# Gate and value products of eight of twelve row blocks in seven-product form, in an attention and SwiGLU kernel on one core

## The chip, the core and the metric

The kernel runs on one core of a Trainium2 chip. Its engines work side by side and wait for each other by semaphores: TensorE (PE; its weight loads are PEld) multiplies matrices into PSUM banks, ScalarE (ACT) and VectorE (DVE) move and combine what lies in PSUM and SBUF, GpSimd (POOL) here computes on tiles in SBUF alone and issues some DMA, SyncE (SP) issues the other DMA. The "granted clock" is the share of TensorE's full speed that the profile records as granted to it. The metric is the device time of one execution in microseconds, median of several.

## The reference

Linear attention (8 batches, 8 heads, 576 tokens, head size 64) gives x, and a SwiGLU block is applied to it:

```python
q_s = softmax(q, axis=-1);  k_s = softmax(k, axis=2)          # shapes 8, 8, 576, 64
kv  = einsum('bhsd,bhse->bhde', k_s, v)
x   = einsum('bhsd,bhde->bhse', q_s, kv)  -> (4608 tokens, 512)
g   = x @ w_gate                                              # 512 x 1536
out = (g * sigmoid(g) * (x @ w_val)) @ w_out                  # 1536 x 512, fp32
```

## The kernel before

The 1536 hidden features are 12 row blocks of 128; 512 tokens are one chunk. For each row block a unit makes gate and value by eight 512-column matmuls, Silu on ACT, and the product on DVE:

```python
def m_unit(c0, n, m):
    ...
    for w, nm in ((wg, "g_ps"), (wv, "u_ps")):
        ps = [f_tile(nm) for _ in parts]
        for kk in range(KT):                                  # KT = 4
            for p_, (c, w_) in zip(ps, parts):
                nc.tensor.matmul(out=p_[:, 0:w_], lhsT=w[:, kk, ms], rhs=xt[:, kk, c:c + w_], ...)
    ...
        nc.scalar.activation(out=sg[:, 0:w_], in_=g_ps[:, 0:w_], func=AF.Silu)
        nc.vector.tensor_mul(hr[:, m, r:r + w_], sg[:, 0:w_], u_ps[:, 0:w_])
```

The output product already has seven-product form (Strassen's scheme in Winograd's variant): `o_quad` needs seven block products instead of eight, four sums of the weights (`w_sums`, once, on POOL) and four sums of h in each chunk:

```python
def h_sum(Q, i, ...):          # a[t][c]: token half t, feature half c of h
    if i == 0:   eng.tensor_add(s[0], a[1][0], a[1][1])
    elif i == 1: eng.tensor_sub(s[1], s[0], a[0][0])
    elif i == 2: eng.tensor_sub(s[2], a[0][0], a[1][0])
    else:        eng.tensor_sub(s[3], a[0][1], s[1])
```

In the kernel before, the four h sums stand on DVE behind the units 0 to 3, one each, and the chunk's attention work stands between other units. The kernel's PSUM pool has eight buffers, called banks in what follows, and every PSUM tile takes one. Names in the traces below: `qs` is the softmax of q, `kv` the product of keys and values, `kn` the same, normalised, `xa` and `xz` the banks in which x arises, `xt` x in SBUF, `vb` the 16-bit copy of v.

The softmax here doesn't subtract the row's maximum and nothing guards it: scores larger than these inputs give would overflow.

## Time and profile before

| | before |
|---|---|
| median of 3 runs | 310.19 us (309.98 to 310.38) |
| span of the profiled run | 308.0 us |
| PE / DVE / ACT / POOL busy | 98 / 66 / 47 / 18 % |
| one 512-token chunk with attention | 31.9 us |

From the page of the kernel before, the table of busy time (us, share of the span, instructions) and the chain of waits (share of the span of each engine on the chain that ended last):

```profile
PE 302.4 (98%) x2200; PEld 183.1 (59%) x2200; DVE 204.1 (66%) x395; ACT 144.1 (47%) x232; POOL 55.7 (18%) x42
...
PE 93%; DVE 4%; DMA 1%; ACT 0%; issue 0%
```

TensorE bounds it, nearly without a gap. The timeline of the kernel before, PE alone, gives the price of a matmul (columns: start, duration, engine, line, operation, output and inputs, shapes, count; us):

```profile
120.82 1.47 PE L383 MATMUL ox<-wt,hr 128*128 128x256 f16 x12
122.13 1.03 PE L304 MATMUL g_ps<-xt,wg 128*128 128x512 bf16 x4
122.99 1.03 PE L304 MATMUL u_ps<-xt,wv 128*128 128x512 bf16 x4
```

Read starts, not durations, since the ends are modelled and overlap. Twelve matmuls of 256 columns take 122.13 - 120.82 = 1.31 us, 109 ns each; four of 512 take 0.865 us, 216 ns each. Per column they cost the same, so fewer columns is less time.

Timeline of the kernel before, DVE and POOL only, where h sums on DVE met POOL; the last line is an h sum that met nothing:

```profile
74.22 3.09 POOL L351 TENSOR_TENSOR wt<-wo,wt 128x1536 f16<-128x1536 f16 x1
...
76.78 1.34 DVE L361 TENSOR_TENSOR hs<-hr 128x1536 bf16<-128x1536 bf16 x1
...
77.26 1.87 POOL L112 CAST vb<-v 128x1152 bf16<-128x1152 f32 x1
...
78.65 1.29 DVE L363 TENSOR_TENSOR hs<-hs,hr 128x1536 bf16<-128x1536 bf16 x1
...
79.72 1.23 POOL L112 CAST vb<-v 128x1152 bf16<-128x1152 f32 x1 [0.59 <-DMA v<-in_v_dram]
...
80.46 1.29 DVE L365 TENSOR_TENSOR hs<-hr 128x1536 bf16<-128x1536 bf16 x1
...
108.66 0.95 DVE L361 TENSOR_TENSOR hs<-hr 128x1536 bf16<-128x1536 bf16 x1
```

Add start and duration. POOL ends at 77.31, the sum at 78.12; POOL at 79.13, the sum at 79.94; POOL at 80.95, the sum at 81.75. Each time DVE ends 0.80 to 0.81 us after POOL, whenever it began. Two engines that shared a rate would not give a constant; one that waits for the other's end does. The four later h sums of this profile that met POOL (from 112.11, 143.98, 175.85 and 207.72 us) also ended 0.81 us after it. In the other direction, the cast at 77.26 ends 1.01 us after the DVE sum at 78.12.

### The profile page before, as it was taken

Reading aid. Unit: us, or ns where it says so; the run is one execution under the profiler, and the core shown is the slowest. Engines: PE = TensorE matmul, PEld = TensorE weight load, DVE = VectorE, ACT = ScalarE, POOL = GpSimd, SP = SyncE. Lnnn points to the kernel's source line nnn. Section 1 sums busy time; section 2 is a strip of 40 time slices with the busy share of each in tenths; the row PEclk is TensorE's granted clock in tenths of the full one; section 3 lists DMA queues with packets and bytes.
Section 4 is the critical chain, followed back from the end, with each engine's and each line's share of the span. In section 5 each row is a group of like instructions: output and inputs, shape, how many; then the busy total and the mean of one; then the engine's idle time right before and its main releaser. Section 6 shows DMA issues by size and latency. Waiting matters only on the chain.

```text
span 308.0 us, 5679 instructions
## 1 busy us (share of the span) xinstructions
PE 302.4 (98%) x2200; PEld 183.1 (59%) x2200; DVE 204.1 (66%) x395; ACT 144.1 (47%) x232; POOL 55.7 (18%) x42
## 2 busy tenths in 40 slices
PE   8999999999999999999999999999999999999994
PEld 6777855454675458455844485448544764485443
DVE  3944459967867886788687768776877653664422
ACT  4753387824493439333944385347634213322300
POOL 1840014189420121102020302020200000000000
PEclk9999999999999999999999999999999999999999
DMA  7999999749019910894089506960540050006014
GB/s 262 263 185 207 250 393 391 221 89 393 24 31 203 385 59 0 177 321 180 0 165 294 217 2 144 285 247 2 119 97 0 0 121 19 0 2 136 3 34 103
DMA packets 39180, 46.39 MB, mean 151 GB/s; under 512 B 16368, under 2 KB 22384, under 8 KB 39152
## 3 DMA queue, kind: packets, MB, share of 16 engines
q1 hardware_dynamic: 33104, 41.17, 45.6%
q0 software_dynamic: 5808, 4.72, 9.8%
q8 instruction: 17, 0.28, 0.4%
q10 hardware_dynamic: 240, 0.13, 0.2%
q14 instruction: 11, 0.09, 0.1%
HBM read 37.75 MB, written 9.44 MB: 153 GB/s over the span
## 4 chain that ended last, share of the span: by engine, by line
PE 93%; DVE 4%; DMA 1%; ACT 0%; issue 0%
PE g_ps L304 31%; PE u_ps L304 30%; PE ox L383 12%; PE ow L383 6%; PE o_ps L331 5%; PE oy L383 3%; PE kv L190 3%; DMA q<-in_q_dram 1%; DVE rs L137 1%; PE o_ps L445 1%; PE xa L272 1%; DVE qs L146 1%; DVE xt L232 0%; DVE qt L112 0%; PE xz L272 0%; ACT eq L121 0%
## 5 line engine op out<-in xcount | busy, mean ns | idle before, releaser
L312 ACT ACTIVATE sg<-g_ps 128x512 f32<-128x512 f32 (+2 forms) x120 | 65.1, 554 | 124.3 <-PE g_ps L304 116.9
L313 DVE TENSOR_TENSOR hr<-sg,u_ps 128x512 bf16<-128x512 f32 (+2 forms) x120 | 74.2, 631 | 60.9 <-PE u_ps L304 60.4
L304 PE MATMUL g_ps<-xt,wg 128*128 128x512 bf16 (+2 forms) x480 | 111.6, 358 | 0.2
L304 PE MATMUL u_ps<-xt,wv 128*128 128x512 bf16 (+2 forms) x480 | 111.0, 358 | 0.0
L304 PEld LDWEIGHTS <-wv 128*128 128x128 f16 x480 | 46.9, 98 | 46.9 <-issue 0.3
L304 PEld LDWEIGHTS <-wg 128*128 128x128 f16 x480 | 45.9, 98 | 44.8 <-issue 2.2
L112 POOL CAST vb<-v 128x1152 bf16<-128x1152 f32 x14 | 19.6, 1398 | 103.5 <-DMA v<-in_v_dram 42.2
L383 PEld LDWEIGHTS <-hs 128*128 128x128 bf16 x336 | 32.9, 98 | 3.8
L383 PEld LDWEIGHTS <-hr 128*128 128x128 bf16 x252 | 24.7, 98 | 4.3
L137 DVE TENSOR_REDUCE rs<-eq 128x18 f32<-128x1152 bf16 x16 | 21.5, 1346 | 6.3 <-ACT eq L121 6.3
L146 POOL TENSOR_TENSOR qs<-eq,rr 128x1152 bf16<-128x1152 bf16 x7 | 14.8, 2121 | 58.2 <-DVE rr L141 49.1
L383 PE MATMUL ox<-wt,hs 128*128 128x256 f16 x168 | 20.6, 273 | 0.0
L121 ACT ACTIVATE eq<-q 128x1152 bf16<-128x1152 f32 x16 | 18.0, 1158 | 2.7 <-DMA q<-in_q_dram 2.6
L121 ACT ACTIVATE ek<-k 128x1152 bf16<-128x1152 f32 x16 | 18.0, 1152 | 2.0 <-DMA k<-in_k_dram 2.0
L331 PE MATMUL o_ps<-wo,hr 128*128 128x512 f16 x84 | 18.8, 379 | 0.0
L214 DVE TENSOR_SCALAR kn<-kv,kvr 64x64 bf16<-64x64 f32 x56 | 15.9, 283 | 1.3
L417 DVE COPY s<-ox 128x256 f32<-128x256 f32 x14 | 5.9, 425 | 12.8 <-PE ox L383 12.8
L146 DVE TENSOR_TENSOR qs<-eq,rr 128x1152 bf16<-128x1152 bf16 x9 | 13.5, 1498 | 0.4 <-DVE rr L141 0.2
L331 PEld LDWEIGHTS <-hr 128*128 128x128 bf16 x84 | 8.1, 98 | 9.5 <-issue 0.2
L255 PE MATMUL warm_ps<-zero 128*128 128x256 bf16 x80 | 11.2, 307 | 1.1 <-DVE zero L464 1.1
L190 PEld LDWEIGHTS <-ek 64*128 64x128 bf16 x288 | 8.4, 94 | 3.6 <-issue 2.5
L255 PEld LDWEIGHTS <-zero 128*128 128x128 bf16 x80 | 8.6, 110 | 3.1 <-DVE zero L464 1.1
(61 smaller groups left out, 230.8 us busy)
## 6 DMA issues: line engine op xcount, KB each, us to landing
q<-in_q_dram SPq DMA_DIRECT2D x16, 576.0 KB, 7.1
k<-in_k_dram SPq DMA_DIRECT2D x16, 576.0 KB, 8.5
v<-in_v_dram SPq DMA_DIRECT2D x16, 576.0 KB, 9.5
out_dram<-o_sb SPq DMA_DIRECT2D x70, 128.0 KB, 2.4
wo<-in_moe_w_out_dram POOLq DMA_DIRECT2D x3, 512.0 KB, 18.0
wg<-in_moe_w_gate_dram POOLq DMA_DIRECT2D x2, 512.0 KB, 11.1
wv<-in_moe_w_val_dram POOLq DMA_DIRECT2D x2, 512.0 KB, 12.8
wg<-in_moe_w_gate_dram POOLq DMA_DIRECT2D x2, 256.0 KB, 5.3
```

Source lines behind the costliest of these rows:

```text
L112: eng.tensor_copy(out=out, in_=in_)
L121: nc.scalar.activation(out=s["e" + what], in_=raw[what, b, G].rearrange("p h (t d) -> p t h d", d=64), func=AF.Exp,)
L137: nc.vector.reduce_sum(out=rs, in_=s["eq"].rearrange("p t h d -> p (t h) d"), axis=mybir.AxisListType.X)
L146: eng.tensor_mul(s["qs"].rearrange("p t (h d) -> p (t h) d", d=64), s["eq"].rearrange("p t h d -> p (t h) d"), s["rr"].to_broadcast([128, ...
L190: nc.tensor.matmul(out=s["kv"][g][:, 0:129], lhsT=s["ek"][r, t, :, :].rearrange("p h d -> p (h d)"), rhs=s["vb"][r, t, 0:129], start=(t == 0),
L214: nc.vector.tensor_scalar_mul(out_, src, sc)
L255: nc.tensor.matmul(out=ps[:, 0:256], lhsT=zero[:, 0:128], rhs=zero, start=True, stop=True)
L304: nc.tensor.matmul(out=p_[:, 0:w_], lhsT=w[:, kk, ms], rhs=xt[:, kk, c:c + w_], start=(kk == 0), stop=(kk == KT - 1),)
L312: nc.scalar.activation(out=sg[:, 0:w_], in_=g_ps[:, 0:w_], func=AF.Silu)
L313: nc.vector.tensor_mul(hr[:, m, r:r + w_], sg[:, 0:w_], u_ps[:, 0:w_])
L331: nc.tensor.matmul(out=o_ps, lhsT=hr[:, m, r0:r0 + 128], rhs=wo[:, m, :], start=(m == 0), stop=(m == MT - 1),)
L383: nc.tensor.matmul(out=dst[p][:, 0:HN], lhsT=lhs(kk, p), rhs=rhs(kk), start=start and kk == 0, stop=kk == HM - 1, skip_group_check=True,)
```

## The change

The intent is to do to gate and value what `o_quad` does to the output: token halves (t = 0, 1) and halves of the 512 inputs make the left operand, halves of the inputs and gate | value the right one. Seven products of two row blocks cost 7 x 4 matmuls of 256 columns, where direct form costs 16 of 512, that is one eighth less. Four "cycles" a chunk each do two row blocks so, and weave one direct row block in, so that ACT and DVE have time to empty the banks. Cut to its core:

```diff
-    xt = const.tile([128, KT, n_tok], BF16, name="xt", tag="xt")
+    xt = const.tile([128, KT, XR], FP16, name="xt", tag="xt")          # XR = 1536, a ring
+    gt = const.tile([128, 4, 2, SD], FP16, name="gt", tag="gt")        # weight sums
+    xs = [const.tile([128, 2, 256], FP16, ...) for i in range(4)]      # x sums
...
+    def g_sums(eng):        # four differences of gate and value weights, 128x2048 each
+    def x_sum(c0, i, eng=nc.vector):   # four sums of x, 128x512 each
+    def cycle(c0, n, mid=None, slot=None, late=None):
+        prod(bx, wg[:, 0:2], xa(0, 0), True)
+        nc.scalar.copy(out=s1, in_=bx)
+        prod(by, wg[:, 2:4], xa(0, 1), True)
+        prod(bw, gt[:, 0], xs[0], True)
+        nc.scalar.copy(out=s5, in_=bw)
+        flush()                                  # last product of the cycle before
+        nc.vector.tensor_add(s1, by, s1)
+        nc.scalar.activation(out=sa, in_=s1, func=AF.Silu)
+        ... mid(), slot()
+        direct(wg, g_ps)
+        prod(bx, gt[:, 1], xs[1])
+        nc.scalar.copy(out=s2, in_=bx)
+        nc.scalar.activation(out=sd, in_=g_ps, func=AF.Silu)
+        prod(bw, wv[:, 2:4], xs[3])
+        nc.vector.tensor_add(s2, bw, s2)
+        nc.gpsimd.tensor_mul(h_out(0), halves(sa), halves(s2))
+        direct(wv, u_ps)
+        prod(bx, gt[:, 2], xs[2])
+        nc.vector.tensor_add(s5, bx, s5)
+        nc.vector.tensor_mul(hr[:, md, rh:rh + 512], sd, u_ps)
+        ... late()
+        def last():
+            prod(bx, gt[:, 3], xa(1, 1))
+            nc.scalar.activation(out=sb, in_=bx, func=AF.Silu)
+            nc.gpsimd.tensor_mul(h_out(1), halves(sb), halves(s5))
+        pend.append(last)
...
     def o_quad(Q, between):
         ... first output product
+        between(-1)                              # flush()
         ... second output product
...
+        w_adds = g_sums(nc.vector)               # in the 448-token chunk:
+            if 4 <= m < 8:
+                w_adds[m - 4]()
...
+            def sums_h():
+                for i, eng in enumerate((nc.vector, nc.vector, nc.gpsimd, nc.gpsimd)):
+                    h_sum(ci, i, eng=eng)
+            cycle(c0, 0, slot=sums_h)
+            o_quad(ci, between)
+            cycle(c0, 1, slot=norm_1 if att else None)
+            cycle(c0, 2, mid=(lambda: kv_pair(b)) if att else None)
+            cycle(c0, 3, late=sums_x if ci + 1 < n_ch else None)
```

Left out of the cut: `kn` is made by one instruction for a 128x128 block, one `qs` multiply a chunk goes from DVE to POOL, v is loaded into two buffers instead of three, and in the 448-token chunk the x products stand one row block earlier.

The bank `bx` collects four products in turn. The "flushed product" is the last of them. It may start only when DVE's `s5` add has read the bank.

More of the change, by code (lines that the diff above doesn't have):

```diff
@@ L49 @@
     HN = d_model // 2
+    XR = 1536
+    NS = 4
+    SD = 2 * NS * 128
     WARM = (64, 8, 8)
@@ L54 @@
     at = ctx.enter_context(tc.tile_pool(name="at", bufs=2))
-    ff = ctx.enter_context(tc.tile_pool(name="ff", bufs=3))
+    ff = ctx.enter_context(tc.tile_pool(name="ff", bufs=4))
     ob = ctx.enter_context(tc.tile_pool(name="ob", bufs=5))
-    sn = ctx.enter_context(tc.tile_pool(name="sn", bufs=1))
+    sn = ctx.enter_context(tc.tile_pool(name="sn", bufs=2))
     psp = ctx.enter_context(tc.tile_pool(name="psp", bufs=8, space=bass.MemoryType.PSUM))
@@ L67 @@
     hs = const.tile([128, 4, HM, 256], BF16, name="hs", tag="hs")
-    xt = const.tile([128, KT, n_tok], BF16, name="xt", tag="xt")
+    xt = const.tile([128, KT, XR], FP16, name="xt", tag="xt")
+    gt = const.tile([128, 4, 2, SD], FP16, name="gt", tag="gt")
+    xs = [const.tile([128, 2, 256], FP16, name=f"xs{i}", tag=f"xs{i}") for i in range(4)]
     hr = const.tile([128, MT, RING], BF16, name="hr", tag="hr")
@@ L76, in load @@
     def load(b, G, what, src, after=None):
-        raw[what, b, G] = ld.tile([128, 2, T * 64], FP32, tag=what, name=what)
+        raw[what, b, G] = ld.tile(
+            [128, 2, T * 64], FP32, tag=what, name=what, bufs=2 if what == "v" else 3
+        )
         ap = bass.AP(
@@ L206, in kn, with ring_parts, put_x @@
         if "kn" not in s:
-            s["kn"] = at.tile([128, 2, 64], BF16, tag="kn", name="kn")
-        for h in range(2):
-            r = slice(64 * h, 64 * h + 64)
-            out_, src, sc = s["kn"][r, g, :], s["kv"][g][r, r], s["kvr"][r, g:g + 1]
-            if eng is nc.scalar:
-                nc.scalar.mul(out_, src, sc)
-            else:
-                nc.vector.tensor_scalar_mul(out_, src, sc)
+            s["kn"] = at.tile([128, 2, 128], BF16, tag="kn", name="kn")
+        out_, src, sc = s["kn"][:, g, :], s["kv"][g][:, 0:128], s["kvr"][:, g:g + 1]
+        if eng is nc.scalar:
+            nc.scalar.mul(out_, src, sc)
+        else:
+            nc.vector.tensor_scalar_mul(out_, src, sc)
+    def ring_parts(c0, n, ring):
+        c1 = c0 + n
+        while c0 < c1:
+            w_ = min(c1, (c0 // ring + 1) * ring) - c0
+            yield c0 % ring, w_
+            c0 += w_
+    def put_x(eng, k0, c0, src):
+        o = 0
+        for r, w_ in ring_parts(c0, src.shape[-1], XR):
+            copy(eng, xt[:, k0, r:r + w_], src[:, o:o + w_])
+            o += w_
     def x(b, G, piece, eng=nc.scalar):
@@ L225, in x @@
                     out=xp[h][64 * g:64 * g + 64, 0:n].rearrange("p (t c) -> p t c", c=64),
-                    lhsT=s["kn"][r, g, :],
+                    lhsT=s["kn"][r, g, r],
                     rhs=s["qt"][g][r, t0:t1, :],
@@ L230, in x @@
         c0 = b * S + 64 * t0
-        copy(eng, xt[:, 2 * G, c0:c0 + n], xp[0][:, 0:n])
-        nc.vector.tensor_copy(out=xt[:, 2 * G + 1, c0:c0 + n], in_=xp[1][:, 0:n])
+        put_x(eng, 2 * G, c0, xp[0][:, 0:n])
+        put_x(nc.vector, 2 * G + 1, c0, xp[1][:, 0:n])
     def x_both(b, G, eng=nc.scalar):
@@ L273, in x_pair @@
                             out=o[64 * g:64 * g + 64, :].rearrange("p (t c) -> p t c", c=64),
-                            lhsT=s["kn"][r, g, :],
+                            lhsT=s["kn"][r, g, r],
                             rhs=s["qt"][g][r, t0:t1, :],
@@ L278, in x_pair @@
             for h, eng in ((0, nc.scalar), (1, nc.vector)):
-                copy(eng, xt[:, 2 * G + h, c0:c0 + n_a], ps[G][h][:, 0:n_a])
+                put_x(eng, 2 * G + h, c0, ps[G][h][:, 0:n_a])
         for h, eng in ((0, nc.scalar), (1, nc.vector)):
-            copy(
-                eng,
-                xt[:, h:h + 2 * NG - 1:2, c0 + n_a:c0 + S],
-                z[h].rearrange("p (g c) -> p g c", g=NG),
-            )
+            o = 0
+            for r, w_ in ring_parts(c0 + n_a, n_z, XR):
+                copy(
+                    eng,
+                    xt[:, h:h + 2 * NG - 1:2, r:r + w_],
+                    z[h].rearrange("p (g c) -> p g c", g=NG)[:, :, o:o + w_],
+                )
+                o += w_
     def kv_pair(b):
@@ L304, in m_unit @@
                     nc.tensor.matmul(
-                        out=p_[:, 0:w_], lhsT=w[:, kk, ms], rhs=xt[:, kk, c:c + w_],
+                        out=p_[:, 0:w_], lhsT=w[:, kk, ms], rhs=xt[:, kk, c % XR:c % XR + w_],
                         start=(kk == 0), stop=(kk == KT - 1),
@@ L313, in m_unit, with flush @@
             nc.vector.tensor_mul(hr[:, m, r:r + w_], sg[:, 0:w_], u_ps[:, 0:w_])
+    pend = []
+    def flush():
+        while pend:
+            pend.pop()()
+    def g_sums(eng):
+        b11, b12 = wg[:, 0:2, 0:SD], wv[:, 0:2, 0:SD]
+        b21, b22 = wg[:, 2:4, 0:SD], wv[:, 2:4, 0:SD]
+        return [
+            lambda: eng.tensor_sub(gt[:, 0], b12, b11),
+            lambda: eng.tensor_sub(gt[:, 1], b22, gt[:, 0]),
+            lambda: eng.tensor_sub(gt[:, 2], b22, b12),
+            lambda: eng.tensor_sub(gt[:, 3], b21, gt[:, 1]),
+        ]
@@ new lines, in x_sum, with halves, prod, direct @@
+    def x_sum(c0, i, eng=nc.vector):
+        r = c0 % XR
+        a11, a12 = xt[:, 0:2, r:r + 256], xt[:, 2:4, r:r + 256]
+        a21, a22 = xt[:, 0:2, r + 256:r + 512], xt[:, 2:4, r + 256:r + 512]
+        if i == 0:
+            eng.tensor_add(xs[0], a21, a22)
+        elif i == 1:
+            eng.tensor_sub(xs[1], xs[0], a11)
+        elif i == 2:
+            eng.tensor_sub(xs[2], a11, a21)
+        else:
+            eng.tensor_sub(xs[3], a12, xs[1])
+    def cycle(c0, n, mid=None, slot=None, late=None):
+        r, rh = c0 % XR, c0 % RING
+        m0, md = 2 * n, 2 * NS + n
+        def halves(t):
+            return t.rearrange("p (j c) -> p j c", j=2)
+        def prod(bank, wgt, rhs, first=False):
+            for j in range(2):
+                c = slice(128 * (m0 + j), 128 * (m0 + j) + 128)
+                for kk in range(2):
+                    nc.tensor.matmul(
+                        out=bank[:, 256 * j:256 * j + 256], lhsT=wgt[:, kk, c], rhs=rhs[:, kk, :],
+                        start=first and j == 0 and kk == 0, stop=kk == 1, skip_group_check=True,
+                    )
+        def direct(w, ps):
+            for kk in range(KT):
+                nc.tensor.matmul(
+                    out=ps, lhsT=w[:, kk, 128 * md:128 * md + 128], rhs=xt[:, kk, r:r + 512],
+                    start=(kk == 0), stop=(kk == KT - 1),
+                )
+        def xa(t, c):
+            return xt[:, 2 * c:2 * c + 2, r + 256 * t:r + 256 * t + 256]
+        def h_out(t):
+            return hr[:, m0:m0 + 2, rh + 256 * t:rh + 256 * t + 256]
+        def sg_tile():
+            return ff.tile([128, 512], FP32, tag="sg", name="sg")
+        bx, by, bw = [f_tile(n_) for n_ in ("sx", "sy", "sw")]
+        s1, s2, s5 = [sn.tile([128, 512], FP32, tag=n_, name=n_) for n_ in ("s1", "s2", "s5")]
+        prod(bx, wg[:, 0:2], xa(0, 0), True)
[5 more added lines that the diff above has]
+        nc.vector.tensor_add(s1, by, s1)
+        sa = sg_tile()
+        nc.scalar.activation(out=sa, in_=s1, func=AF.Silu)
+        if mid is not None:
+            mid()
+        if slot is not None:
+            slot()
+        g_ps, u_ps = f_tile("g_ps"), f_tile("u_ps")
+        direct(wg, g_ps)
+        prod(bx, gt[:, 1], xs[1])
+        nc.scalar.copy(out=s2, in_=bx)
+        sd = sg_tile()
+        nc.scalar.activation(out=sd, in_=g_ps, func=AF.Silu)
[6 more added lines that the diff above has]
+        nc.vector.tensor_mul(hr[:, md, rh:rh + 512], sd, u_ps)
+        if late is not None:
+            late()
+        def last():
+            prod(bx, gt[:, 3], xa(1, 1))
+            sb = sg_tile()
+            nc.scalar.activation(out=sb, in_=bx, func=AF.Silu)
+            nc.gpsimd.tensor_mul(h_out(1), halves(sb), halves(s5))
+        pend.append(last)
@@ L372, in o_quad @@
         s1, s2, s5 = [
-            [sn.tile([128, HN], FP32, tag=f"{n}{p}", name=n) for p in range(2)]
-            for n in ("s1", "s2", "s5")
+            [t[:, HN * p:HN * p + HN] for p in range(2)]
+            for t in [sn.tile([128, 512], FP32, tag=n, name=n) for n in ("s1", "s2", "s5")]
         ]
@@ L549 @@
         exp(2, 1, "k")
-        chunks = [(S, 448)] + [(c, 512) for c in range(1024, n_tok, 512)]
-        for ci, (c0, n) in enumerate(chunks):
-            b = ci + 2
-            steps = {}
-            if b < B:
-                steps = {8: lambda: kv_pair(b), 10: lambda: x_pair(b)}
+        w_adds = g_sums(nc.vector)
+        for m in range(MT):
+            if m == 4:
+                norm_sum(2, 1)
+                norm_mul(2, 1, nc.gpsimd)
+                tr_dma(2, 1)
+                load_group(3, 0)
+                load_group(3, 1)
+            m_unit(S, 1024 - S, m)
+            if m == 5:
+                w_sums(nc.gpsimd)
+            if m == 8:
+                kv_pair(2)
+            if m == 9:
+                x_pair(2)
+            if 4 <= m < 8:
+                w_adds[m - 4]()
+        for i in range(4):
+            x_sum(1024, i)
+        n_ch = n_tok // 512 - 1
+        for ci in range(1, n_ch):
+            b, c0 = ci + 2, 512 * (ci + 1)
+            att = b < B
             def between(i):
-                if b >= B:
-                    return
-                if i == 0:
+                if i < 0:
+                    flush()
+                elif att and i == 0:
                     for G in range(NG):
@@ L565, in between, with norm_1, sums_x @@
                         cast_v(b, G, nc.gpsimd)
-                else:
+                elif att:
                     norm_sum(b, 0)
                     norm_mul(b, 0, nc.gpsimd)
-            for m in range(MT):
-                if ci == 0 and m == 4:
-                    norm_sum(2, 1)
-                    norm_mul(2, 1, nc.gpsimd)
-                    tr_dma(2, 1)
-                    load_group(3, 0)
-                    load_group(3, 1)
-                if ci > 0 and m == 4:
-                    o_quad(ci, between)
-                    if b < B:
-                        tr_dma(b, 0)
-                if ci > 0 and m == 5 and b < B:
-                    norm(b, 1)
-                    tr_dma(b, 1)
-                    if b + 1 < B:
-                        load_group(b + 1, 0)
-                        load_group(b + 1, 1)
-                m_unit(c0, n, m)
-                if ci == 0 and m == 5:
-                    w_sums(nc.gpsimd)
-                if ci > 0 and m < 4:
-                    h_sum(ci, m)
-                if m in steps:
-                    steps[m]()
+            def sums_h():
+                for i, eng in enumerate((nc.vector, nc.vector, nc.gpsimd, nc.gpsimd)):
+                    h_sum(ci, i, eng=eng)
+            def norm_1():
+                norm_sum(b, 1)
+                norm_mul(b, 1, nc.gpsimd)
+                tr_dma(b, 1)
+                if b + 1 < B:
+                    load_group(b + 1, 0)
+                    load_group(b + 1, 1)
+            def sums_x():
+                for i in range(4):
+                    x_sum(c0 + 512, i)
+            cycle(c0, 0, slot=sums_h)
+            o_quad(ci, between)
+            if att:
+                tr_dma(b, 0)
+            cycle(c0, 1, slot=norm_1 if att else None)
+            cycle(c0, 2, mid=(lambda: kv_pair(b)) if att else None)
+            if att:
+                x_pair(b)
+            cycle(c0, 3, late=sums_x if ci + 1 < n_ch else None)
+        flush()
         last = n_tok // 128 - 4
```

## The prediction

> **What bounds the kernel now.** TensorE: the page gives PE 302.4 of 308.0 us (98%), the chain of waits is 93% PE, at full granted clock. Timeline: four 512-column matmuls take 0.865 us, twelve 256-column ones 1.31 us (109 ns each; the 98 ns weight loads hide). A 512-token chunk with attention takes 31.9 us: 24 x 0.865 gate/value, 9.17 output products, 1.8 attention.
>
> **What the change removes.** In each of seven 512-token chunks eight row blocks cost 4 x 28 x 0.109 = 12.2 us instead of 13.8: 11.3 us in all. Without stalls: 299 us.
>
> **What it adds.** ACT: PSUM copies (0.58 each). DVE: adds (0.69), four x sums a chunk (estimate 0.45 each), four weight sums (estimate 1.2 each, from 0.95 for 1536). POOL: multiplies (estimate 1.05, from 3.09 for 1536) and half of the h sums (3.09 each).
>
> **Why I expect a loss.** The Trainium skill, "SBUF — State Buffer", section "Who interferes with whom", says a DVE instruction with two SBUF inputs and a GpSimd instruction reading SBUF exclude each other for a whole instruction. It agrees here: four h sums on DVE that met a busy POOL ended 0.80 to 0.81 us after POOL's op (1.34, 1.29, 1.29, 1.04 us instead of 0.95), and POOL casts that met DVE ended 1.0 us after it (1.87 to 2.01 instead of 1.14). Multiplies with one PSUM input did not slow.
>
> 1. Remainder chunk (448 tokens): four weight sums on DVE stand between the multiplies of row blocks 4 to 7 while POOL runs its four 3.09 us output-weight sums. They alternate, each holding DVE up to 4 us. PSUM banks come free late, and the kn products behind them hold back the x products: about 13 us of TensorE stall, plus 2 to 3 us at a lower clock after a 7 us gap.
> 2. Later chunks, cycle 0: flushed product, ACT Silu (0.6), POOL multiply (1.05); then POOL takes its h sum (3.09) before DVE's first h sum, which waits for it; only after two h sums come DVE's adds s2 and s5. The product flushed inside the output products needs s5: 4.0 us late, six chunks.
> 3. The x sums stand behind cycle 3's last multiply: the next chunk's third product waits 1.3 us.
> 4. Cycle 1: two table loads (1.28) and four exps leave ACT late for the s2 copy: 0.8 us; elsewhere 0.4.
>
> All of it is critical: TensorE runs in order. A full chunk: 30.1 + 1.3 + 4.0 + 1.2 = 36.6 us, against 31.9. Total: 13 to 15 (1) + 0.6 (first seven-product chunk) + 4 x 4.8 + 2 x 3.8 + 2 (final flush, clock) = 43 to 45 us; I shade it to 40.
>
> **Predicted: 350 us, 80% range 328 to 366. Faster by over 2%: 0.07; within 2%: 0.05; slower by over 2%: 0.88.**
>
> **What would show it.** PE busy 86 to 90%. Step 1: DVE weight sums of 2 to 4 us, TensorE waits of several us at 68 to 85 us. Step 2: the first h sum on DVE about 3.9 us long, the flushed product waiting 4 us for s5. Step 3: 1.3 us waits for the first x sum. Chunks of 36 to 37 us. Matmuls unchanged.
>
> **What would make it wrong.** DVE getting the port before POOL's h sum: step 2 shrinks to about 1.3 us, the whole lands near 325. Both locks absent: about 308. Gaps lowering the clock everywhere: over 366.

## The result, and the profile after

| | before | after |
|---|---|---|
| median | 310.09 us (4 runs) | 357.35 us (4 runs, 356.54 to 359.54) |
| ratio | | 1.153 (95% interval 1.148 to 1.159): slower |
| PE / DVE / ACT / POOL busy | 98 / 66 / 47 / 18 % | 86 / 65 / 52 / 51 % |
| mean granted clock | 1.00 | 0.957 |
| one chunk with attention | 31.9 us | 38.0 us (37.97 to 39.14 in four chunks) |

Ratios here and below are the mean time of one kernel's fast runs over that of the other's fast runs of the same rounds, so not quite the ratio of the medians quoted.

Page of the changed kernel, the same two lines as before, and the granted clock in tenths over 40 slices between them:

```profile
PE 306.4 (86%) x2536; PEld 220.8 (62%) x2536; DVE 231.1 (65%) x411; ACT 185.5 (52%) x315; POOL 181.5 (51%) x117
...
PEclk9999999978999989998999879998999899989999
...
PE 62%; DVE 14%; issue 7%; ACT 5%; POOL 5%; DMA 4%; SPq 1%; DVEq 0%; POOLq 0%; ACTq 0%
```

TensorE is busy no less, though it has fewer columns to do, because part of its work now runs at a lower clock; and 48 us of the span it is idle. The view of waits of the changed kernel, PE alone, says for what (us in total, times, longest):

```profile
PE sx L376 <- DVE s L423: 24.3, 7, 3.9
PE xa L290 <- DVE kn L219: 7.1, 1, 7.1
PE sw L376 <- DVE xs L357: 5.8, 7, 0.9
PE sx L376 <- ACT s L415: 2.7, 5, 0.5
PE g_ps L325 <- DVE hr L334: 1.5, 1, 1.5
```

The first line is the flushed product waiting for s5, the second and fifth the 448-token chunk, the third the x sums, the fourth the s2 copy of cycle 1. How the first comes about, in the timeline of the changed kernel (PE, DVE, POOL) through cycle 0 of one chunk and the start of its output products; brackets give idle time before and what ended it:

```profile
119.52 1.27 POOL L432 TENSOR_TENSOR hr<-sg,s 128x512 bf16<-128x512 f32 x1 [2.63 <-ACT sg L431]
...
120.74 3.09 POOL L486 TENSOR_TENSOR hs<-hr 128x1536 bf16<-128x1536 bf16 x1
120.82 3.83 DVE L482 TENSOR_TENSOR hs<-hr 128x1536 bf16<-128x1536 bf16 x1 [1.49 <-POOL hr L432]
...
121.57 1.47 PE L504 MATMUL ox<-wo,hr 128*128 128x256 f16 x12
...
124.68 0.96 DVE L484 TENSOR_TENSOR hs<-hs,hr 128x1536 bf16<-128x1536 bf16 x1
125.56 0.68 DVE L419 TENSOR_TENSOR s<-sw,s 128x512 f32<-128x512 f32 x1
...
126.16 0.68 DVE L423 TENSOR_TENSOR s<-sx,s 128x512 f32<-128x512 f32 x1
...
126.89 1.01 PE L376 MATMUL sx<-xt,gt 128*128 128x256 f16 x4 [3.85 <-DVE s L423]
127.70 2.77 PE L504 MATMUL ow<-wt,hs 128*128 128x256 f16 x12
```

POOL's multiply ends at 120.79. Its next instruction, the third h sum, begins at once; DVE's first h sum, which waited for the same multiply, begins 0.08 us later and ends at 124.65, which is 0.82 us after POOL's end at 123.83. DVE's instructions start in the order of the program, so both adds stand behind it (125.56 and 126.16), and TensorE waits 3.85 us. DVE shows "busy" for those 3.83 us; nothing in the busy share tells that it is blocked. Last line: the next twelve matmuls need 2.56 us (to the following start at 130.26) instead of 1.31, so the wait also cost clock.

The 448-token chunk of the changed kernel, DVE and POOL, shows the same lock among the weight sums:

```profile
62.37 2.12 POOL L153 TENSOR_TENSOR qs<-eq,rr 128x1152 bf16<-128x1152 bf16 x1 [3.61 <-DVE rr L148]
...
62.61 2.96 DVE L346 TENSOR_TENSOR gt<-wv,wg 128x2048 f16<-128x2048 f16 x1
...
64.45 4.06 POOL L469 TENSOR_TENSOR wt<-wo 128x1536 f16<-128x1536 f16 x1
...
66.02 3.58 DVE L347 TENSOR_TENSOR gt<-wv,gt 128x2048 f16<-128x2048 f16 x1
...
68.59 3.95 POOL L470 TENSOR_TENSOR wt<-wo,wt 128x1536 f16<-128x1536 f16 x1
...
70.05 3.58 DVE L348 TENSOR_TENSOR gt<-wv 128x2048 f16<-128x2048 f16 x1
```

The ends alternate: POOL 64.49, DVE 65.57, POOL 68.51, DVE 69.60, POOL 72.54, DVE 73.63. Each instruction runs only when the other engine's is done. Behind these sums stand the multiplies that free PSUM banks and the kn products that x needs. The seven-product stage starts at 84.43 us, where the kernel before starts its first 512-token chunk at 74.18. Part of this is clock: after the wait of 7.1 us four matmuls of 448 columns took 1.46 us and the next four 1.15 us, by their starts, instead of 0.76.

### The profile page after: what moved, and what is told of

Same layout as the page of the kernel before. It is cut to its first block, busy times and chain, and to the rows that moved or that the text cites. A ratio compares the mean times of both kernels' runs of the same rounds, so it can differ in the third digit from the quotient of the medians.

```text
span 354.8 us, 6505 instructions
## 1 busy us (share of the span) xinstructions
PE 306.4 (86%) x2536; PEld 220.8 (62%) x2536; DVE 231.1 (65%) x411; ACT 185.5 (52%) x315; POOL 181.5 (51%) x117
## 4 chain that ended last, share of the span: by engine, by line
PE 62%; DVE 14%; issue 7%; ACT 5%; POOL 5%; DMA 4%; SPq 1%; DVEq 0%; POOLq 0%; ACTq 0%
PE sx L376 10%; PE ox L504 9%; PE ow L504 7%; DVE hs L482 6%; PE g_ps L325 6%; PE u_ps L325 6%; PE o_ps L452 5%; PE g_ps L383 4%; PE sw L376 4%; DMA v<-in_v_dram 3%; PE oy L504 3%; PE sy L376 2%; PE u_ps L383 2%; DVE s L419 2%; POOL hr L420 2%
## 5 line engine op out<-in xcount | busy, mean ns | idle before, releaser
L376 PEld LDWEIGHTS <-gt 128*128 128x128 f16 x448 | 43.6, 99 | 54.1 <-issue 29.7
L432 POOL TENSOR_TENSOR hr<-sg,s 128x512 bf16<-128x512 f32 x28 | 35.6, 1272 | 40.3 <-ACT sg L431 40.3
L420 POOL TENSOR_TENSOR hr<-sg,s 128x512 bf16<-128x512 f32 x28 | 35.6, 1272 | 34.9 <-DVE s L419 34.9
L376 PE MATMUL sx<-xs,gt 128*128 128x256 f16 x224 | 33.6, 272 | 2.7 <-ACT s L415 2.7
L488 POOL TENSOR_TENSOR hs<-hr,hs 128x1536 bf16<-128x1536 bf16 x7 | 21.6, 3093 | 17.5 <-DVE hs L484 17.5
L482 DVE TENSOR_TENSOR hs<-hr 128x1536 bf16<-128x1536 bf16 x7 | 23.9, 3416 | 9.0 <-POOL hr L432 9.0
L383 PE MATMUL g_ps<-xt,wg 128*128 128x512 f16 x112 | 28.8, 379 | 0.0
L383 PE MATMUL u_ps<-xt,wv 128*128 128x512 f16 x112 | 28.7, 379 | 0.0
L325 PE MATMUL g_ps<-xt,wg 128*128 128x320 f16 (+2 forms) x144 | 25.8, 314 | 1.7 <-DVE hr L334 1.5
L325 PE MATMUL u_ps<-xt,wv 128*128 128x320 f16 (+2 forms) x144 | 25.2, 311 | 0.0
L376 PEld LDWEIGHTS <-wg 128*128 128x128 f16 x224 | 21.8, 98 | 4.4 <-issue 0.9
```

The lines of the kernel that those rows point to most:

```text
L376: nc.tensor.matmul(out=bank[:, 256 * j:256 * j + 256], lhsT=wgt[:, kk, c], rhs=rhs[:, kk, :], start=first and j == 0 and kk == 0, stop=kk ...
L383: nc.tensor.matmul(out=ps, lhsT=w[:, kk, 128 * md:128 * md + 128], rhs=xt[:, kk, r:r + 512], start=(kk == 0), stop=(kk == KT - 1),)
L420: nc.gpsimd.tensor_mul(h_out(0), halves(sa), halves(s2))
L432: nc.gpsimd.tensor_mul(h_out(1), halves(sb), halves(s5))
```

## The experiments

The theory: DVE instructions with two SBUF inputs and POOL instructions exclude each other, and the order in which they come makes TensorE wait; the seven-product form itself costs what was reckoned. Rivals: the waits are the plain latency of a long chain; DVE or POOL simply has too much work; the waits hide each other, so that removing one brings nothing. All edits are to the changed kernel.

| label | edit | median us | ratio to before |
|---|---|---|---|
| (the change) | | 357.35 | 1.153 |
| a_swap | POOL's two h sums in the other order | 335.63 | 1.083 |
| h_dve | all four h sums on DVE | 348.09 | 1.124 |
| b_gsum | weight sums moved to where POOL is idle | 351.71 | 1.136 |
| d_xs0 | first x sum earlier | 348.97 | 1.125 |
| fill | matmuls on zeros in the wait | 346.27 | 1.118 |
| abd | a_swap, b_gsum and d_xs0 together | 319.31 | 1.030 |
| abdew | and two more orders | 313.14 | 1.009 |
| gbdew | and h sums placed anew | 304.07 | 0.981 |
| best | and the flushed product later | 301.29 | 0.972 |

### a_swap: who gets the port

```diff
-                for i, eng in enumerate((nc.vector, nc.vector, nc.gpsimd, nc.gpsimd)):
+                for i, eng in ((0, nc.vector), (1, nc.vector), (3, nc.gpsimd), (2, nc.gpsimd)):
                     h_sum(ci, i, eng=eng)
```

> Edit: POOL computes its two h sums in the other order, the one that needs DVE's second h sum first, so POOL cannot take the SBUF port before DVE has done its two; nothing else changes, POOL and DVE do the same work. Theory (the port is exclusive and POOL's 3.09 us sum got it first): DVE's first h sum falls from 3.83 to about 0.95 us, the flushed product waits about 1.1 us for the s5 add instead of 3.85, the lower clock after that wait vanishes, the third output product may wait 0.6 us for POOL's late sum: about 20 us off, 334 to 340 us. Rival (the wait is the latency of the chain flushed product, Silu, POOL multiply, two h sums, two adds in DVE's order, whatever POOL does meanwhile): the first h sum and the wait stay, about 357 us.

Measured: 335.63 us, 21.7 us off, within the theory's range. The timeline of this kernel (DVE, POOL, PE), the same place in the same chunk:

```profile
121.74 1.28 POOL L432 TENSOR_TENSOR hr<-sg,s 128x512 bf16<-128x512 f32 x1 [2.63 <-ACT sg L431]
...
123.06 0.96 DVE L482 TENSOR_TENSOR hs<-hr 128x1536 bf16<-128x1536 bf16 x1 [1.50 <-POOL hr L432]
...
125.18 3.10 POOL L488 TENSOR_TENSOR hs<-hr,hs 128x1536 bf16<-128x1536 bf16 x1 [2.16 <-DVE hs L484]
...
126.26 0.60 PE L376 MATMUL sx<-xt,gt 128*128 128x256 f16 x4 [0.99 <-DVE s L423]
126.69 1.47 PE L504 MATMUL ow<-wt,hs 128*128 128x256 f16 x12
```

The first h sum takes 0.96 us, the wait is 0.99 us, and the matmuls after it run at full clock. No work was taken away; two POOL instructions changed places. That is what latency alone cannot explain. A rest of about 1 us stays: two h sums of 0.96 us still stand in front of the adds. One wait came new: POOL's late sum holds an output product 0.6 us (4.0 us in seven chunks), the size expected; in the order of the timeline it is the fifth product, not the third.

### h_dve: is it too much work on one of them?

```diff
-                for i, eng in enumerate((nc.vector, nc.vector, nc.gpsimd, nc.gpsimd)):
+                for i, eng in enumerate((nc.vector,) * 4):
```

> Edit: all four h sums on DVE, POOL has none. Theory (exclusive port): no sum meets POOL, each takes 0.95 us, but four stand in front of s2 and s5, so the flushed product still waits about 2.85 us[...]: 341 to 347 us, better than the change, worse than the swapped order. Rival (DVE has simply too much work in cycle 0): worse than the change, over 357 us. Second rival (POOL's volume of work is what hurts): as good as or better than the swapped order, under 338 us.

Measured: 348.09 us, 1 us above the expected range. All sums take 0.95 to 0.96 us, and the flushed product waits 2.72 us, close to the 2.85 expected. So without any lock, four sums in front of the adds still hurt: the lock and the place in DVE's order both count. DVE's volume of work is not the point, for the run is faster than the change although DVE has two more sums in each chunk. POOL's is not either, for POOL without any h sum is slower than POOL with two in the better order. What was off is the clock. The expectation counted on full clock behind a gap of this length; it fell after four of the six gaps of 2.7 us:

```profile
128.81 0.60 PE L376 MATMUL sx<-xt,gt 128*128 128x256 f16 x4 [2.72 <-DVE s L423]
129.24 2.40 PE L504 MATMUL ow<-wt,hs 128*128 128x256 f16 x12
...
165.66 0.60 PE L376 MATMUL sx<-xt,gt 128*128 128x256 f16 x4 [2.73 <-DVE s L423]
166.09 1.47 PE L504 MATMUL ow<-wt,hs 128*128 128x256 f16 x12
```

(Timeline of this kernel, PE, two chunks: 2.40 us against 1.47 for the same twelve matmuls after the same wait.)

### b_gsum: the weight sums

```diff
         for m in range(MT):
             m_unit(0, S, m)                      # first chunk, POOL idle
+            if m >= 8:
+                w_adds[m - 8]()
...
-            if 4 <= m < 8:                       # 448-token chunk
-                w_adds[m - 4]()
```

> Edit: the four weight sums on DVE go from row blocks 4 to 7 of the 448-token chunk, where POOL runs its output-weight sums, to row blocks 8 to 11 of the first chunk, where POOL is idle. Theory (exclusive port in the 448-token chunk): weight sums take 1.2 us each instead of 3.0 to 3.6, POOL's output-weight sums 3.09 instead of 4.06, the waits of 7.1 and 1.5 us and the low clock around 80 us vanish: about 10 us off, 345 to 349 us. Rival (the gap comes from placing the kv and x products one row block earlier, or from the weight sums' own time on DVE): little changes, over 354 us.

Measured: 351.71 us; 5.6 us off, less than expected. The mechanism holds: the weight sums take 1.22 us each, POOL's output-weight sums 3.08 to 3.10, the waits of 7.1 and 1.5 us are gone, and the x products still stand one row block earlier than in the kernel before (the kv products did not move, although the expectation says so), so that rival falls. The stage of seven products starts 10.9 us earlier (73.55 against 84.43), but at its first flushed product the lead is 6.0 us (84.56 against 90.58): part of the gain went into a new collision of the same kind. The 448-token chunk now ends sooner, while POOL is still at its sums, and the x sums meet it (timeline of this kernel, DVE, POOL and PE; the first two lines are a weight sum and an output-weight sum that met nothing):

```profile
34.47 1.22 DVE L346 TENSOR_TENSOR gt<-wv,wg 128x2048 f16<-128x2048 f16 x1
...
64.32 3.08 POOL L469 TENSOR_TENSOR wt<-wo 128x1536 f16<-128x1536 f16 x1
...
73.58 3.09 POOL L472 TENSOR_TENSOR wt<-wo,wt 128x1536 f16<-128x1536 f16 x1
...
74.36 2.59 DVE L357 TENSOR_TENSOR xs<-xt 128x512 f16<-128x512 f16 x1
...
77.10 1.01 PE L376 MATMUL sw<-xs,gt 128*128 128x256 f16 x4 [2.51 <-DVE xs L357]
```

An x sum that meets nothing takes 0.42 us. So 2.5 us of waiting came back at the next place where DVE needed two SBUF inputs, and the clock fell behind it (1.01 us for the four matmuls shown, 0.60 at full clock).

### d_xs0: is a removed wait gained, or passed on?

```diff
-            cycle(c0, 3, late=sums_x if ci + 1 < n_ch else None)
+            cycle(c0, 3, slot=sum_x0 if more else None, late=sums_x if more else None)   # sums 1 to 3 stay late
```

> Edit: the first x sum of the next chunk is computed in cycle 3 after that cycle's s1 add, not behind its last multiply; the other three stay. Theory (TensorE waits 0.9 us a chunk for a sum that stands late in DVE's order): the six waits vanish and nothing else moves: 5 to 6 us off, 351 to 353 us. Rival (the wait is only passed on, because the flushed product's wait for s5 grows by as much): 356 to 358 us, with that wait at about 4.7 us.

Measured: 348.97 us, 8.4 us off, more than expected. The six waits are gone, the flushed product's wait is unchanged at 3.85 us, so nothing was passed on. In the trace, from the flushed product of cycle 2 to that of cycle 3 takes 4.78 us instead of 5.87: 1.09 us in six chunks is 6.5 us. Of the other 2 us one is within the noise: the two profiled runs differ by 7.3 us (356.54 and 349.24), and the changed kernel's four runs spread over 3.0 us. The rest is not settled. In this profile one of the six long waits did not lower the clock, where all six did in the changed kernel's; but the mean granted clock is no higher (0.955 against 0.957), so that does not explain it.

### fill: what the clock costs

```diff
                 if i < 0:
+                    if ci > 1:
+                        warm_up(30)              # 30 matmuls on zeros, result unused
                     flush()
```

> Edit to the changed kernel: 30 matmuls on zeros (30 x 0.109 = 3.3 us, result unused) stand in front of the flushed product in the output products, in the chunks where it waits 3.85 us; no useful work moves. Theory (each long wait also lowers the granted clock, and the matmuls after it take about double for 2 to 3 us): the wait shrinks to about 0.6 us with the product starting at the same moment, the matmuls after it take 109 ns, about 1.4 us less in each of six chunks: 347 to 351 us, although TensorE does 20 us more. Rival (the low clock costs nothing, or zeros don't hold it up): 356 us or more.

Measured: 346.27 us, 11.1 us off: a little better than expected, although 180 useless matmuls were added. The timeline of this kernel, PE:

```profile
123.25 3.44 PE L273 MATMUL warm_ps<-zero 128*128 128x256 bf16 x30
127.26 0.60 PE L376 MATMUL sx<-xt,gt 128*128 128x256 f16 x4 [0.58 <-DVE s L423]
127.69 1.47 PE L504 MATMUL ow<-wt,hs 128*128 128x256 f16 x12
```

The product starts no earlier relative to its chunk, but what follows runs at 109 ns a matmul. A full chunk takes 36.4 us (127.26 to 163.63) instead of 38.0 (37.97 to 39.14). So 1.6 us or more a chunk, some 10 of the 47 us lost, was clock that the waits brought with them. It is a test, not a remedy: the remedy is to have no wait.

### abd and abdew: do the causes add up?

abd is the three edits a_swap, b_gsum and d_xs0 in one.

> Edit: the swapped POOL order, the early weight sums and the early first x sum together. Theory (three separate causes that add): 335.6 less 7 (early weight sums; 5.6 alone, where the first x sum of the first seven-product chunk met POOL and waited 2.5 us) less 6.5 (0.9 to 1.1 us in six chunks): 320 to 325 us. Rival (the three hide the same wait): no better than 330 us.

Measured: 319.31 us, 38.0 us off, 0.7 us below the expected range. Alone they brought 21.7, 5.6 and 8.4, together 35.7. They are separate causes and add, within the 3.0 us over which the changed kernel's runs spread. abdew has two more edits:

```diff
+        if s2_first:                              # cycle 1: Silu, and its table load, behind the s2 copy
+            nc.scalar.activation(out=sa, in_=s1, func=AF.Silu)
...
         cast_v(2, 1, nc.gpsimd)
+        w_sums(nc.gpsimd, 0)                      # first output-weight sum ahead of POOL's qs multiply
...
-                w_sums(nc.gpsimd)
+                w_sums(nc.gpsimd, 1)              # the other three where all four stood
```

> Edit: the same, and in cycle 1 ACT copies s2 before its Silu table load and Silu, and POOL does the first of its four output-weight sums before, not after, the qs multiply, so that it is done when the first x sums come. Expected: 0.54 us less in each of five chunks, about 2 us less at the first seven-product chunk: 315 to 319 us. Rival for both (the delay is passed on to the next wait): within 1 us of the run without them.

Measured: 313.14 us, 6.2 us off, 2 us below the expected range. The two edits were run together, so what each brought is read from the waits alone. The waits for the s2 copy are gone, and the wait for the first x sum of the first seven-product chunk fell from 2.3 to 0.3 us. That wait had lowered the clock in abd (PEclk 8 in its slice); from here on PEclk is 9, the highest digit, in all slices, and the mean granted clock of the profiled runs is 1.00. Two waits are left: for s5 (6.7 us in seven times) and for POOL's late h sum (4.0 us).

### gbdew and best: versions that beat both kernels

gbdew is abdew with the h sums placed so that each is ready when it is needed and none meets POOL's sum:

```diff
         nc.vector.tensor_add(s2, bw, s2)
+        h_sum(ci, 0)                              # DVE, cycle 0 only
         nc.gpsimd.tensor_mul(h_out(0), halves(sa), halves(s2))
...
         nc.vector.tensor_add(s5, bx, s5)
+        h_sum(ci, 1); h_sum(ci, 2)                # DVE
+        h_sum(ci, 3, eng=nc.gpsimd)
```

> Edit: the same, but the h sums stand elsewhere: DVE does s2 add, first h sum, s5 add, second and third h sum, last multiply; POOL only the fourth. Theory (what is left of the loss is the 1.1 us wait for s5 and the 0.6 us wait for POOL's late sum): both vanish in six or seven chunks, a full chunk takes 30.5 to 31 us, below the 31.9 of the kernel before: 304 to 309 us, the saved TensorE time shows at last. Rival (DVE has no room for a third sum): over 313 us.

Measured: 304.07 us, ratio 0.981 (0.979 to 0.982). The time saved on TensorE shows at last, and DVE, which does a third sum, has room. A chunk takes 30.7 to 31.3 us. The wait for s5 is 0.34 us in six chunks, not quite nothing, and 0.85 us at the end. best moves the flushed product:

```diff
-        between(-1)                               # behind the first output product
         ... second output product, its s5 copies
+        between(-1)
...
-        flush()
         last = n_tok // 128 - 4
+        o_unit(last)
+        flush()
```

> Edit to the best version so far (304.07 us): the flushed product stands behind the second output product instead of the first, and the last one behind the first 128 output rows. Theory (0.34 us of wait for s5 in six chunks and 0.85 us at the end are all of it that is left): 301 to 302.5 us, no wait for s5 over 0.1 us. Rival (the Silu and POOL multiply behind it come later and something else waits): 304 us or more.

Measured: 301.29 us (301.12 to 301.60), ratio 0.972 (0.971 to 0.974) to the kernel before, correct. Page and view of waits (PE) of this kernel:

```profile
PE 292.6 (98%) x2536; PEld 215.5 (72%) x2536; DVE 212.5 (71%) x418; ACT 184.6 (62%) x315; POOL 165.0 (55%) x110
```

```profile
PE warm_ps L273 <- DVE zero L595: 1.1, 1, 1.1
PE xa L290 <- DMA qtd<-qs: 0.8, 2, 0.6
PE sx L376 <- ACT xt L117: 0.5, 3, 0.2
```

TensorE is at 98% again, with 9.8 us less to do than before (292.6 against 302.4), and no wait over 1.1 us. The stall-free estimate of the prediction was 299 us. A chunk of this kernel takes 30.5 to 31.2 us, where the prediction's sum has 30.1 without stalls.

## Why the prediction was right

Predicted 350 us (328 to 366), slower with a probability of 0.88; measured 357.35. The matmuls cost what was reckoned, and the loss came from where the sums were put. That the total came so close is in part luck: step 1 was taken some 5 us too large, the clock behind the other waits some 8 us too small.

- **What is removed, 11.3 us.** Right for the price, a little high for the gain. Matmuls of 256 columns cost 109 ns in every kernel here at full clock; best, almost without waits, has 9.8 us less PE busy time and is 8.8 us faster than the kernel before. Where the rest went was not followed up.
- **The exclusive port.** Right, read from four sums in the profile before, and shown by a_swap.
- **Step 1, 13 us and 2 to 3 more of clock.** The mechanism was right, the size too large. The seven-product stage began 10.3 us late (84.43 against 74.18), against 15 to 16 predicted; of this the clock is about 1.1 us (from 1.46 and 1.15 against 0.76). The first weight sum came at 62.6 us, one multiply earlier than I had reckoned (65.4, a figure that the recorded prediction does not give); that this is why the loss was smaller is not shown. Predicted sums of 2 to 4 us, measured 2.96 to 3.58.
- **Step 2, 4.0 us, six chunks.** Measured 3.85 us, six times, and the first h sum 3.83 us against 3.9.
- **Step 3, 1.3 us.** Measured 0.91 us of wait, worth 1.09 us when removed.
- **Step 4, 0.8 us in five chunks, 0.4 elsewhere.** Measured 0.54 us for the copy in five chunks; the other short waits in such chunks, for ACT's copies of x, are 0.17 us, four times.
- **A full chunk, 36.6 us.** Measured 38.0 to 39.1. The waits were a little shorter than reckoned, and yet the chunk is longer, because one term above all was mis-sized: "2 (final flush, clock)" for all clock losses outside step 1. The clock fell after each of the six waits of 3.85 us, some 10 us by fill. I had named gaps that lower the clock everywhere as what would push the time over 366. They did so after every long wait, and the time stayed under 366.
- **The shading.** The sum was 43 to 45 us of loss, and I shaded it to 40 for no measured reason. The loss is 47.
- **The cases named as what would make it wrong.** DVE first at the port was put near 325 us; a_swap, which is this case, measured 335.63: the gain was 21.7 us against 25, and its start was 7 us higher. Both locks absent was put at 308; abd, where both are moved apart and the first x sum is earlier too, is at 319.31, though one x sum still meets POOL there.

## What to carry to other kernels

Before moving work to POOL, list the DVE instructions with two SBUF inputs that will run beside it: they exclude each other for whole instructions, and a 3 us POOL sum in front of a 1 us DVE sum holds everything behind it in DVE's order. A change of order can be worth more than the work itself: swapping two POOL instructions brought 21.7 us, and the same seven-product form was 15% slower or 2.8% faster than the kernel before, by order and placement alone. When one such wait is removed, look where the next two instructions of that kind will now meet, and count long TensorE waits above their length, since the clock may fall with them.

## What the Trainium skill lacked or had wrong

- "SBUF — State Buffer", section "Who interferes with whom": right, and it decided the prediction. It says that an instruction can measure several times slower so; what it does not say is that a profile counts the blocked instruction as busy for all that time (a DVE sum of 0.95 us shown as 3.83 us, weight sums of 1.22 us as 2.96 to 3.58 us), so busy shares hide it. Nor does it say who comes next when both engines have instructions queued: here they alternated, one instruction each, through four DVE and four POOL sums.
- "TensorE: Matmul & The Clock Gate", section "HAM oscillation — how this bites in real kernels", gives the rule "no PE-idle gaps >~3.4µs". Here the clock also fell after four of six gaps of 2.72 us (h_dve) and after one of 2.51 us (b_gsum), and it held after one of the six gaps of 3.85 us in another run (d_xs0). Gaps of 0.99 us never lowered it. The rule does not say that matmuls on zeros hold it up; here 30 of them in a gap did.
- "ScalarE: Activation LUTs", section "What ACT_TABLE_LOAD costs", gives 1283 ns and a drain of 1380 ns, 2.66 us for a switch. The load agrees (1.28 us); no drain is seen: in the changed kernel the copy before the Silu load ended at 139.01 us and the Silu began at 140.31, 1.30 us for the whole switch.
- "GPSIMD Engine Reference", section "Elementwise — side-by-side cycle accounting", times a two-input add only for 2048 fp32 elements (4497 ns, 2.2 ns each). Not there: 16-bit sums of 1536 elements took 3.09 us (2.0 ns each), and multiplies of two fp32 inputs with bf16 output took 1.27 us for 512 (2.5 ns each). I had estimated 1.05 us for these from the 16-bit ones.
